# Expert 0's slots emptied by plain transfers, later counts, and another order of each expert's two layers

## The chip, the core and the metric

The kernel runs on one core of a Trainium2 chip. The metric is the device time of one execution in microseconds (us), lower is better: the median of several timed runs. Beside them stands one execution that was recorded by the hardware profiler. The core's engines are PE (TensorE, the matmuls), PEld (its weight loads), DVE (VectorE), ACT (ScalarE), POOL (GpSimd) and SP (SyncE, which here only issues transfers). Each runs its own instructions in order and waits for others at semaphores.

## What is computed

A retention attention, whose output rows are the tokens of a mixture of eight experts with one expert a token:

```python
scores = scale * np.matmul(q, k.transpose(0, 1, 3, 2))      # 8 x 8 heads x 576 x 576
ret = scores * Dmat                                         # decay gamma[h] ** (i - j), causal
x = np.matmul(ret, v)                                       # -> 4608 tokens x 512
logits = x @ w_gate                                         # 8 experts
e_idx = np.argmax(logits, axis=1)
gate_w = softmax(logits)[e_idx]; eom = sigmoid(x @ w_output_gate)
for e in range(8):
    mask = e_idx == e
    h = np.maximum(x[mask] @ w1[e], 0.0)                    # 512 -> 1024
    out[mask] = gate_w[mask, None] * eom[mask, e, None] * (h @ w2[e])   # 1024 -> 512
```

All inputs and outputs are float32.

## The kernel before

**First stage, retention and routing.** A loop of 36 steps goes over tiles `g` of 128 tokens. A step scales v (`prep`, on POOL, one tile ahead), computes scores (also one tile ahead), the output of the tile before by state and by scores, the state's update, and the rows x of the tile before (`xnat`: two PSUM tiles `xa`, `xb`, copied by ACT into `xgrp`; DVE takes the logits into `lg`). Every fourth tile closes a group `n` of four tiles: `gate1a` to `gate3b` find each row's expert and its slot in a DRAM table `xs` of 8 x 4608 slots of 528 words. POOL then writes each tile's 128 rows into `xs` by an indirect transfer (`scatter_x`, L200). The transfers wait in a list, `todo`, and `scatters` issues them, in most steps one, each behind a small `memset`.

An expert works on 616 slots (`CAP`): 360 in a first part (`CA`, tiles t = 0 to 2 of 128, 128 and 104 rows) and 256 in a second (tiles 3 and 4). A slot that no token has must hold an empty row `zx` whose token number is out of bounds. For experts 1 to 7 `fill` computes, from the count of each expert, which slots are empty, and `fill_slots` writes `zx` there by indirect transfers, five for an expert, after all rows are placed. Expert 0 is needed first, so its first part is read while the last tiles are still computed: in `gate4`, after group 5 (`SNAP`), its slots from the count to 360 are filled by three indirect transfers, and later groups go on from slot 360 (`bump`, `base2`). Again after group 7 three such transfers fill up to 616, and then the last group's rows go over filled slots. So in `gate3a` of the last group the copy of the slots into `sli` (L494) waits until all transfers before it have landed (`gt["after"]`).

**Second stage, the experts.** Matmuls run as three float32r products (high x high, high x low, low x high parts). `mm1(e, part, fb)` makes one of eight blocks of the hidden layer for a part of the slots: 12 matmuls of 360 or 256 columns into a PSUM tile `h_ps`; `hidden` (ACT, then DVE) takes it into `hh`, `hl`. `mm2(e, t)` makes a tile of y: 24 matmuls of 512 columns into `y_ps`, ACT scales it, POOL writes its rows to the output by an indirect transfer. The weights of an expert come in four chunks for each layer by SP through three staging buffers `st`, and ACT and DVE split each into high and low part (`load_w`: `hi_w`, `lo_w`) into buffers that each expert uses anew. The next expert's rows come by SP (`load_x`, four transfers a tile into `x_q`), are transposed on DVE and split by ACT and DVE (`transp_hi`, `transp_lo`).

The order of the second stage is written out by hand, and every engine follows it. Expert 0 goes first part of layer one, y of tiles 0 to 2, second part of layer one, y of tiles 3 and 4. Experts 1 to 7 go first part, second part, y of tiles 0 to 4. Their second-layer chunks are loaded within the first part of layer one, the next expert's rows within the second, and its transposes stand ahead of each y tile. Between the stages the counts of all experts (`c_ps`, a matmul of `cum`, L738) are taken within expert 0's first layer. At the end `overflow_table` computes, on DVE, how many rows did not fit; a loop over them closes the kernel.

Of the kernel before, what the change touches and what calls it, by code (L numbers as in the profile page):

```python
# [24 lines left out]
E = 8  # L25
# [23 lines left out]
def tile_retention_moe(  # L49
# [83 lines left out]
    wpool.tile([P, 48], F32, name="shift1")  # L133
# [30 lines left out]
    scat, todo, fillt = [], [], []  # L164
# [34 lines left out]
    def scatter_x(x, at, bound=None):  # L199
        i = G.indirect_dma_start(out=xs, out_offset=bass.IndirectOffsetOnAxis(ap=at, axis=0), in_=x, in_offset=None,  # L200
                                 **({} if bound is None else dict(bounds_check=bound, oob_is_err=False)))
        tc.declare_no_dep(i.ins, group="xs", reason="the slots written differ, and those read so far get no more")
        tc.add_to_no_dep_group("xs", i.ins)
        scat.append(i.ins)

# [258 lines left out]
    def gate2(ps):  # L464

        n, oh, ex, zs = gt["pend"]
        r_ps = ps[:, 0:GT * E].rearrange("p (t e) -> p t e", t=GT)
        T.matmul(r_ps, lhsT=cbf_sb[:, 0, :], rhs=oh, start=True, stop=False, skip_group_check=True)
        if n > 0:
            T.matmul(r_ps, lhsT=cbf_sb[:, 1, :], rhs=cum.rearrange("p (a e) -> p a e", a=1).broadcast_to([P, GT, E]),  # L470
                     start=False, stop=False, skip_group_check=True)
        for t in range(GT - 1):
            T.matmul(r_ps[:, t + 1:], lhsT=cbf_sb[:, 1, :], rhs=oh[:, t:t + 1].broadcast_to([P, GT - 1 - t, E]),
                     start=False, stop=t == GT - 2, skip_group_check=True)
        c_ps = ps[:, GT * E:GT * E + E]
        if n in (SNAP, NTILE // GT - 2):
            T.matmul(c_ps, lhsT=cbf_sb[:, 1, :], rhs=cum, start=False, stop=False, skip_group_check=True)
            for t in range(GT):
                T.matmul(c_ps, lhsT=cbf_sb[:, 1, :], rhs=oh[:, t], start=False, stop=t == GT - 1, skip_group_check=True)
        gt["ps"] = (r_ps, c_ps)  # L480

    def gate3a():
# [5 lines left out]
        if n in (SNAP, NTILE // GT - 2):  # L488
            V.tensor_copy(cnt[:, 0], c_ps[:, 0:1])
# [4 lines left out]
        i = V.tensor_copy(sli, slf)  # L494
        for j in gt.get("after", ()):
            tc.add_manual_dep(i.ins, j.name, SYNC, reason="the last group's rows go over filled slots")
# [19 lines left out]
    def gate3c():  # L516
# [6 lines left out]
        if n in (SNAP, NTILE // GT - 2):  # L523
            gt["fill"] = n

    def gate4():
        n = gt.pop("fill")
        if n == NTILE // GT - 2:

            V.tensor_tensor(out=cnt[:, 0], in0=cnt[:, 0], in1=bump, op=ALU.add)  # L530
            todo.extend(fill(0, 1, cnt[:, 0:1], lim, CT - TA + 1)[0])
        if n == SNAP:

            todo.extend(fill(0, 1, cnt[:, 0:1], float(CA), TA)[0])
            V.tensor_scalar(out=bump, in0=cnt[:, 0], scalar1=-1.0, scalar2=float(CA), op0=ALU.mult, op1=ALU.add)
            V.tensor_scalar(out=bump, in0=bump, scalar1=0.0, scalar2=None, op0=ALU.max)
            V.tensor_copy(base2, base)
            V.tensor_tensor(out=base2[:, 0, 0:1], in0=base2[:, 0, 0:1], in1=bump, op=ALU.add)
# [50 lines left out]
    def scatters(n, pause):  # L589
        for f in todo[0:n]:  # L590

            G.memset(pause, 0.0)
            f()
        del todo[0:n]

    with tc.manual_schedule():
        S_next = scores(0)
        k_rows(0)
        for g in range(NTILE):
# [5 lines left out]
            if g < NTILE - 4:  # L605
                load(g + 4)
            if g == GT * SNAP + 11:
# [13 lines left out]
            if g < NTILE - 1:  # L621

                scatters(2 if GT * SNAP + 6 < g < GT * SNAP + 11 else 1, gap)
# [26 lines left out]
            if g == NTILE - 1:  # L650
                wide = wk.tile([P, H, D], F32, name="vp")
                gate3c()
                gate4()
# [8 lines left out]
    gt["after"] = list(scat)  # L662
# [74 lines left out]
    c_ps = ps_t.tile([P, 512], F32, name="t_ps")[:, 0:E]  # L737
    T.matmul(c_ps, lhsT=cbf_sb[:, 1, :], rhs=cum, start=True, stop=True)  # L738
    V.tensor_copy(cnt[:, :, 0], c_ps)
    V.tensor_tensor(out=cnt[:, 0], in0=cnt[:, 0], in1=bump, op=ALU.add)  # L740
    fills = fill(0, E, cnt, lim, CT)
    fills[0] = fill(0, 1, cnt[:, 0:1], float(CAP), 1, late=True)[0]
# [11 lines left out]
    w = [start_w(1, 1, fp) for fp in range(2)]  # L754
    fill_slots(1)
    fill_slots(0)
    for fb in range(5, FB):
        mm1(0, 0, fb)
# [8 lines left out]
    load_x(1, 1)  # L767
    for e in range(E):
        nx = e + 1 < E
        for fb in range(FB if e > 0 else 0):  # L770

            mm1(e, 0, fb)
            if fb % 2 == 0:
                load_w(2, e, fb // 2)
        for fb in range(FB):
# [10 lines left out]
            elif nx:  # L786
                if fb < CT:
                    load_x(e + 1, fb)
# [8 lines left out]
        xw = {}  # L797
        for t in range(CT):
            if e > 0 or t >= TA:

                for u in range(CT) if e == 0 and t == TA else (t,) if e else ():
                    if nx:
                        xw[u] = transp_hi(e + 1, u)
                        if u > 0:
                            transp_lo(*xw[u - 1])
                        if u == CT - 1:
                            transp_lo(*xw[u])
# [118 lines left out]
```

## Time and profile before

| | us |
|---|---|
| median of 3 timed runs | 603.85 (603.75, 603.85, 605.16) |
| profiled execution, whole | 600.12 |
| its span, first to last instruction | 598.3 |
| busy in the span: PE / PEld | 586.4 / 525.7 |
| busy in the span: DVE / ACT / POOL | 330.8 / 227.0 / 186.3 |
| granted clock of PE, mean share | 0.996 |

The profiled execution was 3.7 us shorter than the median of the timed runs. The busy time of PE is the union of its matmuls' spans; they are pipelined, and the end of each is modelled, so a new matmul starts long before the one ahead has ended. How fast PE goes is therefore read from the starts: how long a stretch of so many matmuls takes.

### The profile page before, as it was taken

How to read it: one execution, taken by the hardware profiler on the slowest of the kernel's cores; microseconds unless marked ns; L12 is line 12 of the kernel's file. 1: busy time of each engine (PE TensorE's matmuls, PEld its weight loads, DVE VectorE, ACT ScalarE, POOL GpSimd, SP SyncE). 2: the span in 40 equal slices, each digit the busy share in tenths (PEclk: the TensorE clock that was granted, in tenths of full speed). 3: DMA queues.
4: the chain of work that ended last, by engine and by line, in shares of the span. 5: the costliest groups of instructions: out<-in, count | busy, mean ns of one | idle time of the engine just before them, and what ended most of it. 6: DMA issues, size and time to landing. Idle time of an engine off the chain costs nothing. (4 is left out here: it accounts for less than half of the span.)

```text
span 598.3 us, 14014 instructions
## 1 busy us (share of the span) xinstructions
PE 586.4 (98%) x5692; PEld 525.7 (88%) x5692; DVE 330.8 (55%) x731; ACT 227.0 (38%) x502; POOL 186.3 (31%) x235
## 2 busy tenths in 40 slices
PE   8999999999999999999999999999999999999995
PEld 6889899889988999889979987997899799889974
DVE  3589899898641864626543472454355435626410
ACT  4534443334322554325333442443344234325210
POOL 3245555575655551125014102501330110110011
PEclk9999999999999999999999999999999999999998
DMA  8889889886235565326424732453273335421011
GB/s 325 293 288 322 323 299 350 328 307 202 92 118 170 173 219 149 141 67 162 172 86 129 183 122 90 125 163 110 89 181 129 121 97 151 131 77 53 1 42 39
DMA packets 54429, 98.97 MB, mean 165 GB/s; under 512 B 14903, under 2 KB 33336, under 8 KB 54364
## 3 DMA queue, kind: packets, MB, share of 16 engines
q1 hardware_dynamic: 44492, 75.42, 39.0%
q0 software_dynamic: 9440, 21.60, 9.9%
q8 instruction: 45, 0.74, 0.5%
q10 hardware_dynamic: 432, 1.05, 0.5%
q14 instruction: 20, 0.16, 0.1%
HBM read 76.45 MB, written 31.18 MB: 180 GB/s over the span
## 5 line engine op out<-in xcount | busy, mean ns | idle before, releaser
L272 PE MATMUL h_ps<-xh,w1h 128*128 128x256 f32 (+1 forms) x512 | 154.7, 302 | 0.0
L272 PE MATMUL h_ps<-xh,w1l 128*128 128x256 f32 (+1 forms) x512 | 154.5, 302 | 0.0
L272 PE MATMUL h_ps<-xl,w1h 128*128 128x256 f32 (+1 forms) x512 | 154.5, 302 | 0.0
L299 POOL DMA_INDIRECT out_dram<-y,idx x40 | 39.8, 995 | 314.3 <-ACT y L298 268.5
L280 DVE SCALAR_TENSOR_TENSOR hl<-h_ps,hh 128x256 fp32r<-128x256 f32 (+1 forms) x128 | 61.1, 477 | 129.1 <-ACT hh L279 125.7
L293 PE MATMUL y_ps<-w2h,hh 128*128 128x512 f32 (+1 forms) x320 | 125.0, 390 | 0.0
L293 PE MATMUL y_ps<-w2l,hh 128*128 128x512 f32 (+1 forms) x320 | 124.9, 390 | 0.0
L293 PE MATMUL y_ps<-w2h,hl 128*128 128x512 f32 (+1 forms) x320 | 124.7, 390 | 0.0
L279 ACT ACTIVATE hh<-h_ps 128x256 fp32r<-128x256 f32 (+1 forms) x128 | 54.8, 428 | 116.9 <-PE h_ps L272 114.8
L272 PEld LDWEIGHTS h_ps<-xh,w1l 128*128 128x128 f32 x512 | 97.1, 190 | 0.0
L272 PEld LDWEIGHTS h_ps<-xh,w1h 128*128 128x128 f32 x512 | 96.1, 188 | 0.3
L272 PEld LDWEIGHTS h_ps<-xl,w1h 128*128 128x128 f32 x512 | 96.1, 188 | 0.3
L298 ACT ACTIVATE y<-y_ps,idx 128x512 f32<-128x512 f32 (+1 forms) x40 | 27.5, 688 | 138.7 <-issue 90.1
L153 DVE TENSOR_TENSOR w1l<-st,w1h 128x512 fp32r<-128x512 f32 x64 | 47.3, 776 | 48.0 <-ACT w1h L148 46.6
L293 PEld LDWEIGHTS y_ps<-w2h,hl 128*128 128x128 f32 (+1 forms) x320 | 58.8, 184 | 14.1
L293 PEld LDWEIGHTS y_ps<-w2h,hh 128*128 128x128 f32 (+1 forms) x320 | 58.8, 184 | 13.7
L293 PEld LDWEIGHTS y_ps<-w2l,hh 128*128 128x128 f32 (+1 forms) x320 | 58.8, 184 | 13.6
L364 POOL TENSOR_TENSOR vp<-pk,con_sb 128x512 f32<-128x512 f32 x36 | 37.5, 1041 | 52.9 <-PE st_ps L404 37.4
L200 POOL DMA_INDIRECT xs<-xgrp,sli x36 | 39.1, 1087 | 29.8 <-issue 12.9
L200 POOL DMA_INDIRECT xs<-zx,fill x42 | 43.3, 1031 | 7.2 <-issue 6.5
L388 DVE TENSOR_TENSOR S_sb<-sc,con_sb 128x512 f32<-128x512 f32 x64 | 41.0, 682 | 7.4 <-PE sc L377 7.0
L153 DVE TENSOR_TENSOR w2l<-st,w2h 128x512 fp32r<-128x512 f32 x64 | 44.7, 736 | 0.0
(130 smaller groups left out, 676.1 us busy)
## 6 DMA issues: line engine op xcount, KB each, us to landing
st<-in_w_dram SPq DMA_DIRECT2D x64, 512.0 KB
pk<-in_pack_dram SPq DMA_DIRECT2D x32, 768.0 KB
x_q<-xs SPq DMA_DIRECT2D x140, 64.0 KB
kn<-in_krow_dram SPq DMA_DIRECT2D x13, 256.0 KB
pk<-in_pack_dram SPq DMA_DIRECT2D x4, 256.0 KB
pk<-in_pack_dram SPq DMA_DIRECT2D x2, 512.0 KB
x_g<-xs SPq DMA_DIRECT2D x4, 256.0 KB
xs<-zx,fill POOLq DMA_INDIRECT x42, 3.6
```

What stands on the lines that cost most here:

```text
L153: V.tensor_tensor(out=lo[:, k], in0=st[:, k], in1=hi[:, k].bitcast(F32), op=ALU.subtract)
L200: i = G.indirect_dma_start(out=xs, out_offset=bass.IndirectOffsetOnAxis(ap=at, axis=0), in_=x, in_offset=None, **({} if bound is None else ...
L272: i = T.matmul(ps, lhsT=a[:, k, :], rhs=b[:, k, 0:n], start=(j == 0), stop=(j == 3 * KB - 1))
L279: A.activation(out=hh, in_=ps, func=AF.Relu)
L280: V.scalar_tensor_tensor(out=hl, in0=ps, scalar=0.0, in1=hh.bitcast(F32), op0=ALU.max, op1=ALU.subtract)
L293: i = T.matmul(ps, lhsT=a[:, n], rhs=b, start=(j == 0), stop=(j == 3 * FB - 1))
L298: A.activation(out=y, in_=ps, func=AF.Copy, scale=idx.bitcast(F32)[0:m, e, t, 1:2])
L299: G.indirect_dma_start(out=out, out_offset=bass.IndirectOffsetOnAxis(ap=idx[0:m, e, t, 0:1], axis=0), in_=y, in_offset=None, bounds_check= ...
L364: G.tensor_tensor(out=vs[g], in0=pk[g][:, 2].rearrange("p (h d) -> p h d", h=H), in1=gk_sb[:, g % CPB].broadcast_to([P, H, D]), op=ALU.mult)
L388: V.tensor_tensor(out=v(S_sb[:, r].rearrange("p a i -> p (a i)")), in0=v(sc[:, r]), in1=cmat_sb[:, 0:2].rearrange("p c a i -> p a (c i)"). ...
```

## The change

It has two parts. **One:** expert 0's 616 slots are written with `zx` by five plain transfers on SP's queue, in steps 3 to 6, before any row is placed; the first row transfer's `memset` waits for them. The two fills of expert 0 within the first stage go, with the count after group 7 and the wait of `sli`; `scatters` issues one transfer a step. The count after group 5 stays, since `bump` needs it. The counts of all experts, and `fill` for experts 1 to 7, come after the last block of expert 0's first part. **Two:** experts 1 to 7 take the order that expert 0 had: y of tiles 0 to 2 stands between the two parts of layer one. The loads of the next expert's rows move into the first part, its transposes stay ahead of the y tiles, and the last two chunks of its first-layer weights come ahead of tiles 3 and 4 instead of 1 and 3.

```diff
+    def empty_rows(t):
+        n = min(P, CAP - P * t)
+        i = SP.dma_start(out=xs[P * t:P * t + n], in_=zx[0:n])
+        tc.add_to_no_dep_group("xs", i.ins)
+        empty.append(i.ins)
...
-        if n in (SNAP, NTILE // GT - 2):
+        if n == SNAP:
             T.matmul(c_ps, lhsT=cbf_sb[:, 1, :], rhs=cum, start=False, stop=False, skip_group_check=True)
...
-        i = V.tensor_copy(sli, slf)
-        for j in gt.get("after", ()):
-            tc.add_manual_dep(i.ins, j.name, SYNC, reason="the last group's rows go over filled slots")
+        V.tensor_copy(sli, slf)
...
     def gate4():
-        n = gt.pop("fill")
-        if n == NTILE // GT - 2:
-            V.tensor_tensor(out=cnt[:, 0], in0=cnt[:, 0], in1=bump, op=ALU.add)
-            todo.extend(fill(0, 1, cnt[:, 0:1], lim, CT - TA + 1)[0])
-        if n == SNAP:
-            todo.extend(fill(0, 1, cnt[:, 0:1], float(CA), TA)[0])
+        gt.pop("fill")
...
     def scatters(n, pause):
         for f in todo[0:n]:
-            G.memset(pause, 0.0)
+            i = G.memset(pause, 0.0)
+            if not scat:
+                for j in empty:
+                    tc.add_manual_dep(i.ins, j.name, SYNC, reason="rows go over empty ones")
             f()
...
+            for t in {3: (0,), 4: (1,), 5: (2, 3), 6: (4,)}.get(g, ()):
+                empty_rows(t)
...
-                scatters(2 if GT * SNAP + 6 < g < GT * SNAP + 11 else 1, gap)
+                scatters(1, gap)
...
+    for fb in range(5, FB):
+        mm1(0, 0, fb)
     c_ps = ps_t.tile([P, 512], F32, name="t_ps")[:, 0:E]
     T.matmul(c_ps, lhsT=cbf_sb[:, 1, :], rhs=cum, start=True, stop=True)
...
     fill_slots(1)
     fill_slots(0)
-    for fb in range(5, FB):
-        mm1(0, 0, fb)
...
+    def next_x(e, u):
+        xw[u] = transp_hi(e + 1, u)
+        if u - 1 in xw:
+            transp_lo(*xw.pop(u - 1))
+        if u in (TA - 1, CT - 1):
+            transp_lo(*xw.pop(u))
     for e in range(E):
         nx = e + 1 < E
-        for fb in range(FB if e > 0 else 0):
-            mm1(e, 0, fb)
-            if fb % 2 == 0:
-                load_w(2, e, fb // 2)
+        if e > 0:
+            for fb in range(FB):
+                mm1(e, 0, fb)
+                if fb % 2 == 0:
+                    load_w(2, e, fb // 2)
+                elif nx:
+                    load_x(e + 1, fb // 2)
+            for t in range(TA):
+                if nx:
+                    next_x(e, t)
+                    if t == 0:
+                        load_x(e + 1, CT - 1)
+                mm2(e, t)
         for fb in range(FB):
             mm1(e, 1, fb)
...
             elif nx:
-                if fb < CT:
-                    load_x(e + 1, fb)
...
-        for t in range(CT):
-            if e > 0 or t >= TA:
+        for t in range(TA, CT):
+            if nx:
                 for u in range(CT) if e == 0 and t == TA else (t,) if e else ():
...
-                if e and nx and t in (1, 3):
-                    load_w(1, e + 1, 2 + t // 2)
-                mm2(e, t)
+                    next_x(e, u)
+                if e:
+                    load_w(1, e + 1, t - 1)
+            mm2(e, t)
```

Three places show how the instructions stand. **DVE in the step after group 5's slots are known** (`S_sb` are scores of a tile, `xT` its output, `w2l` the low part of a weight chunk). Before:

```order
L388 TENSOR_TENSOR S_sb<-sc,con_sb 128x512 x2
L431 TENSOR_TENSOR xT<-o_ps,gq_sb 128x512
L213 TENSOR_TENSOR fl<-cnt,csm_sb 128x3
L215 TENSOR_SCALAR fo<-fl 128x3
L223 TENSOR_TENSOR fl<-fl,fo 128x3
L224 TENSOR_TENSOR fill_2273<-fl,csm_sb 128x3
L535 TENSOR_SCALAR bump<-cnt 128x1
L536 TENSOR_SCALAR bump<-bump 128x1
L537 COPY base_84<-csm_sb 128x8
L538 TENSOR_TENSOR base_84<-base_84,bump 128x1
L153 TENSOR_TENSOR w2l_1944<-st,w2h_1943 128x512
L555 COPY lg<-xa 128x16
```

and with the change:

```order
L395 TENSOR_TENSOR S_sb<-sc,con_sb 128x512 x2
L438 TENSOR_TENSOR xT<-o_ps,gq_sb 128x512
L534 TENSOR_SCALAR bump<-cnt 128x1
L535 TENSOR_SCALAR bump<-bump 128x1
L536 COPY base_84<-csm_sb 128x8
L537 TENSOR_TENSOR base_84<-base_84,bump 128x1
L153 TENSOR_TENSOR w2l_1949<-st,w2h_1948 128x512
L554 COPY lg<-xa 128x16
```

Four instructions of `fill` are gone from between a tile's `xT` and the copy of the logits `lg`. **PE where the counts of all experts are taken** (`t_ps` receives them; `h_ps` belongs to expert 0's first part). Before:

```order
L272 MATMUL h_ps<-xh_2778,w1h_1014 128x360
L272 MATMUL h_ps<-xl_2779,w1h_1014 128x360
L738 LDWEIGHTS cbf_sb
L738 MATMUL t_ps<-cum,cbf_sb 128x8
L272 MATMUL h_ps<-xh_2778,w1l_1015 128x360
L272 MATMUL h_ps<-xh_2778,w1h_1330 128x360
```

and with the change:

```order
L279 MATMUL h_ps<-xl_2765,w1h_1335 128x360
L279 MATMUL h_ps<-xh_2764,w1l_1336 128x360
L754 LDWEIGHTS cbf_sb
L754 MATMUL t_ps<-cum,cbf_sb 128x8
L300 MATMUL y_ps<-w2h_1632,hh_2916 128x512
L300 MATMUL y_ps<-w2l_1633,hh_2916 128x512
```

The matmul of `cum` stood ahead of the last matmul of block 5; now it stands behind block 7, at the border to y. **PE in expert 1**, at the start of its second part of layer one (matmuls of 256 columns). Before:

```order
L272 MATMUL h_ps<-xl_3551,w1h_3420 128x360
L272 MATMUL h_ps<-xh_3550,w1l_3421 128x360
L272 MATMUL h_ps<-xh_3563,w1h_3154 128x256
L272 MATMUL h_ps<-xl_3564,w1h_3154 128x256
L272 MATMUL h_ps<-xh_3563,w1l_3155 128x256
```

and with the change:

```order
L300 MATMUL y_ps<-w2l_3754,hh_3734 104x512
L300 MATMUL y_ps<-w2h_3753,hl_3735 104x512
L279 MATMUL h_ps<-xh_3523,w1h_3092 128x256
L279 MATMUL h_ps<-xl_3524,w1h_3092 128x256
L279 MATMUL h_ps<-xh_3523,w1l_3093 128x256
```

What stands ahead of the 256-column matmuls was a matmul of 360 columns and is one of 512 columns, as in expert 0 before and after.

## Rows read from the trace of the kernel before

**Rows 1.** The page, section 1: busy us, share of the span, instructions.
```profile
PE 586.4 (98%) x5692; PEld 525.7 (88%) x5692; DVE 330.8 (55%) x731; ACT 227.0 (38%) x502; POOL 186.3 (31%) x235
```
**Rows 2.** PE's waits: line, what it waited for: us, times, longest.
```profile
PE t_ps L738 <- DVE cum L522: 1.1, 1, 1.1
PE xa L546 <- DVE lg L555: 0.8, 1, 0.8
```
**Rows 3.** Busy by stretch in the second stage; columns in the first line.
```profile
core 0: us, PE busy (x) PEld busy (x) DVE busy (x) ACT busy (x) POOL busy (x), PEclk, DMA share, GB/s
160.31:166.33 6.02, 6.02 (x39) 5.88 (x38) 3.18 (x13) 1.82 (x6) 4.96 (x7) 1.00 0.25 93
173.87:184.81 10.94, 10.94 (x51) 9.03 (x49) 1.27 (x7) 1.16 (x2) 9.51 (x13) 1.00 0.63 223
191.26:202.15 10.89, 10.89 (x98) 10.89 (x96) 6.50 (x13) 6.31 (x14) 8.22 (x10) 1.00 0.77 226
213.04:228.40 15.36, 15.36 (x97) 15.36 (x96) 8.21 (x15) 8.09 (x16) 10.64 (x12) 1.00 0.58 166
228.40:239.71 11.31, 11.31 (x99) 11.31 (x97) 5.29 (x11) 4.18 (x10) 0.00 (x0) 1.00 0.49 147
239.71:250.60 10.89, 10.89 (x51) 9.00 (x50) 7.75 (x11) 4.27 (x8) 0.98 (x1) 1.00 0.42 154
552.24:563.55 11.31, 11.31 (x98) 11.27 (x97) 4.08 (x9) 3.16 (x8) 0.00 (x0) 1.00 0.01 1
```
**Rows 4.** Order of time near the last group's slots: start, us, engine, line, [idle before].
```profile
168.20 0.33 PE L272 MATMUL h_ps<-xl,w1h 128*128 128x360 f32 x1
168.42 0.17 DVE L494 CAST sli<-slf 128x4 int32<-128x4 f32 x1 [1.14 <-DMA xs<-zx,fill]
169.63 0.18 PE L738 MATMUL t_ps<-cum,cbf_sb 128*128 128x8 bf16 x1 [1.11 <-DVE cum L522]
```
**Rows 5.** Order of time in the step that has the fill of group 5.
```profile
121.32 1.76 DVE L223 TENSOR_TENSOR fl<-fl,fo 128x3 f32<-128x3 f32 x1
122.00 1.05 POOL L364 TENSOR_TENSOR vp<-pk,con_sb 128x512 f32<-128x512 f32 x1
123.17 0.63 PE L404 MATMUL st_ps<-vp,kn 128*64 128x64 f32 x16
124.33 0.17 DVE L555 COPY lg<-xa 128x16 f32<-128x16 f32 x1
124.55 0.76 PE L546 MATMUL xa<-iw,xT 128*128 128x144 f32 x4 [0.75 <-DVE lg L555]
126.03 0.90 PE L377 MATMUL sc<-pk 64*64 64x128 f32 x32 [0.23 <-DVE S_sb L388]
```
**Rows 6.** Order of time at the count after group 7.
```profile
150.57 0.24 PE L479 MATMUL k_ps<-oh,cbf_sb 128*128 128x8 bf16 x4
```
**Rows 7.** Order of time near the first row transfer, on POOL, PE and ACT.
```profile
39.39 1.15 POOL L200 DMA_INDIRECT xs<-xgrp,sli  x1 [2.62 <-PE o_ps L428]
40.56 1.05 POOL L364 TENSOR_TENSOR vp<-pk,con_sb 128x512 f32<-128x512 f32 x1
44.99 1.09 PE L428 MATMUL o_ps<-S_sb,vp 128*64 128x128 f32 x16
48.77 0.35 ACT L550 COPY xgrp<-xa 128x256 f32<-128x256 f32 x1
```
**Rows 8.** Busy by stretch in the first stage, columns as in rows 3.
```profile
16.00:20.00 4.00, 4.00 (x96) 3.62 (x90) 2.15 (x4) 2.45 (x9) 1.04 (x1) 1.00 1.06 391
20.00:24.00 4.00, 4.00 (x88) 3.53 (x82) 2.33 (x5) 3.34 (x13) 1.04 (x1) 1.00 0.29 81
30.00:33.00 3.00, 3.00 (x65) 2.59 (x59) 2.42 (x7) 1.50 (x6) 1.04 (x1) 1.00 0.55 171
```
**Rows 9.** Order of time in experts 7 and 1: a chunk's last split, SP's row loads.
```profile
551.53 1.30 DVE L153 TENSOR_TENSOR w2l<-st,w2h 128x512 fp32r<-128x512 f32 x2
217.87 9.88 SPq L168 DMA_DIRECT2D x_q<-xs  x20
```

More of the change, by code (lines that the diff above doesn't have):

```diff
@@ L128, in load_rest @@
             G.memset(zx.bitcast(I32)[:, DM:DM + 1], NT)
-    wpool.tile([P, 48], F32, name="shift1")
+    wpool.tile([P, 64], F32, name="shift1")
     W1, W2 = {}, {}
@@ L163, in tile_retention_moe @@
     pe = [None]
-    scat, todo, fillt = [], [], []
+    scat, todo, fillt, empty = [], [], [], []
     pools = {"xt0": xta, "ht0": hpa}
@@ L487, in gate3a @@
         V.tensor_tensor(out=sl, in0=r_ps, in1=bs.broadcast_to([P, GT, E]), op=ALU.add)
-        if n in (SNAP, NTILE // GT - 2):
+        if n == SNAP:
             V.tensor_copy(cnt[:, 0], c_ps[:, 0:1])
@@ L522, in gate3c @@
         V.tensor_tensor(out=cum, in0=cum, in1=ohs, op=ALU.add)
-        if n in (SNAP, NTILE // GT - 2):
+        if n == SNAP:
             gt["fill"] = n
     def gate4():
-        n = gt.pop("fill")
-        if n == NTILE // GT - 2:
-            V.tensor_tensor(out=cnt[:, 0], in0=cnt[:, 0], in1=bump, op=ALU.add)
-            todo.extend(fill(0, 1, cnt[:, 0:1], lim, CT - TA + 1)[0])
-        if n == SNAP:
-            todo.extend(fill(0, 1, cnt[:, 0:1], float(CA), TA)[0])
[L535 to L538, printed above, removed]
+        gt.pop("fill")
+        V.tensor_scalar(out=bump, in0=cnt[:, 0], scalar1=-1.0, scalar2=float(CA), op0=ALU.mult, op1=ALU.add)
+        V.tensor_scalar(out=bump, in0=bump, scalar1=0.0, scalar2=None, op0=ALU.max)
+        V.tensor_copy(base2, base)
+        V.tensor_tensor(out=base2[:, 0, 0:1], in0=base2[:, 0, 0:1], in1=bump, op=ALU.add)
     def xnat(g):
@@ L652, in tile_retention_moe @@
                 gate3c()
-                gate4()
                 scatters(len(todo), wide)
@@ L661, in tile_retention_moe @@
                 transp_lo(*x)
-    gt["after"] = list(scat)
     psctx.close()
@@ L736, in tile_retention_moe @@
     weights_lo(NTILE)
[L737 to L742, printed above, removed]
     rest.__exit__(None, None, None)
@@ L754, in tile_retention_moe @@
     w = [start_w(1, 1, fp) for fp in range(2)]
+    for fb in range(5, FB):
+        mm1(0, 0, fb)
+    c_ps = ps_t.tile([P, 512], F32, name="t_ps")[:, 0:E]
+    T.matmul(c_ps, lhsT=cbf_sb[:, 1, :], rhs=cum, start=True, stop=True)
+    V.tensor_copy(cnt[:, :, 0], c_ps)
+    V.tensor_tensor(out=cnt[:, 0], in0=cnt[:, 0], in1=bump, op=ALU.add)
+    fills = fill(0, E, cnt, lim, CT)
+    fills[0] = fill(0, 1, cnt[:, 0:1], float(CAP), 1, late=True)[0]
     fill_slots(1)
     fill_slots(0)
-    for fb in range(5, FB):
-        mm1(0, 0, fb)
     load_idx(1, 0)
@@ L767, in tile_retention_moe @@
     load_x(1, 1)
+    xw = {}
+    def next_x(e, u):
[4 more added lines that the diff above has]
+            transp_lo(*xw.pop(u))
     for e in range(E):
         nx = e + 1 < E
-        for fb in range(FB if e > 0 else 0):
-            mm1(e, 0, fb)
-            if fb % 2 == 0:
-                load_w(2, e, fb // 2)
+        if e > 0:
[11 more added lines that the diff above has]
+                mm2(e, t)
         for fb in range(FB):
@@ L796, in tile_retention_moe @@
             overflow_table()
-        xw = {}
-        for t in range(CT):
-            if e > 0 or t >= TA:
+        for t in range(TA, CT):
+            if nx:
                 for u in range(CT) if e == 0 and t == TA else (t,) if e else ():
[L802 to L807, printed above, removed]
-                if e and nx and t in (1, 3):
-                    load_w(1, e + 1, 2 + t // 2)
-                mm2(e, t)
+                    next_x(e, u)
+                if e:
+                    load_w(1, e + 1, t - 1)
+            mm2(e, t)
     mctx.close()
```

## The prediction

> **What bounds the kernel now.** I read the page's first section, then PE's waits, then the busy time by stretch, and last the order of time around each wait. The first shows PE busy for 98% of the span [rows 1]; all other engines have room. So only two things can shorten the span: a gap in PE's chain that closes, or a stretch of the same matmuls that takes PE less time. PE's list of waits has few entries, and two of them lie where the change works: 1.1 us for `cum` and 0.8 us for `lg` [rows 2]. No wait at all is listed within experts 1 to 7, so there the reader should look at how long equal stretches take. The clock that PE was granted is 1.00 in every stretch used here [rows 3], the higher of its two levels.
>
> The stretch table holds the surprise. The second part of layer one is 96 matmuls of 256 columns in each expert. In expert 0 they take 10.89 us (113 ns each), in expert 1 and in expert 7 11.31 us (118 ns each) [rows 3]. Experts 2 to 6 read 11.30 or 11.31 in the same view. Code, tiles and clock are the same. It isn't other work in the way: expert 0's stretch is the busiest (DMA share 0.77, POOL 8.22 us) and the fastest, expert 7's the quietest (0.01 and 0) and slow. What differs is what PE did before: in expert 0 a tile of y (512 columns), in the others 360-column matmuls. The first part shows the same kind of thing: 36 matmuls of 360 columns behind 144-column ones of `xnat` take 6.02 us (167 ns each), 96 behind a tile of y take 15.36 us (160 ns each) [rows 3]. I read this as a state that a stretch takes over at its start and keeps: how far the weight loads run ahead of the matmuls. That reading is an inference; the times are measured.
>
> **The change, part by part.**
>
> *The last group's wait goes.* `sli` waited 1.14 us for the last transfer of `zx`; behind it on DVE came the sum into `cum`, for which PE stood still: its matmuls start at 168.20 and then at 169.63 [rows 4]. A normal step is 0.16 us, so 1.27 us are lost. Without fills in the list `sli` waits for nothing that is late, and the matmul of `cum` now comes behind block 7, 25 steps of 0.16 us or 4 us after the place where `cum` was late by 1.3 us. What is late next is nothing on PE: the blocks need only `xh`, `xl` and PSUM tiles freed long before. The move has no price of its own, since the matmul interrupts the stream once in either place. Gain 1.27 us; at least 1.1, the listed wait.
>
> *The fill after group 5 goes.* In this step DVE spends 1.76 us on `fl<-fl,fo`, a copy of 3 columns, while POOL scales a tile beside it [rows 5]. That pushes the logits' copy to 124.33, and PE, done with its state update at 123.80 (123.17 + 0.63), starts `xa` only at 124.55 and waits 0.23 us once more for the scores' tile [rows 5]. The instruction goes with three others. Then `lg` comes at 122.6 or earlier, 1.2 us ahead of PE. Gain 0.75 + 0.23 = 0.98 us. Four instructions for `bump` stay; should one of them be held for 1.6 us in the same way, `lg` comes at 124.2 and 0.2 us of the gain are left. I take 0.98, since in this step POOL now issues one transfer fewer and scales its tile earlier.
>
> *Five small matmuls after group 7 go.* Four of them span 0.24 us with their pipeline [rows 6]; I take 0.1 us.
>
> *Five plain writes come, 1.3 MB in steps 3 to 6.* At the 391 GB/s that this stage reaches they are 3.3 us of transfer. The queue has room: the DMA share is 0.29 in the four us from 20 and 0.55 in the three from 30, which leaves 2.8 + 1.4 = 4.2 us [rows 8]. Behind them on SP stand the loads of tiles and weight chunks; on POOL, behind the first `memset` that now waits, stand the first row transfer and the scaling for tile 9. That transfer began at 39.39 and the scaling ended at 41.61; PE needs it at 44.99, and ACT overwrites the transferred rows at 48.77 [rows 7]. So the writes may land up to 3.4 us later than the first transfer used to begin before PE sees it. The room exceeds the writes, so I take 0; bound 0 to 2 us of loss.
>
> *Fewer transfers on POOL.* Six row transfers and their memsets leave POOL's queue. POOL is not waited for there, so nothing by itself.
>
> *The counts and fills of all experts come later.* They need `cum` and DVE, and POOL then writes the slots of expert 1 while PE makes y of tiles 0 to 2. These transfers were bound by POOL, busy 9.51 of 10.94 us in that stretch [rows 3], and its row transfers ahead of them now start earlier. Their reader is the load of expert 1's rows, which PE needs at 213.04 [rows 3], almost 30 us after that stretch. I take 0.
>
> *The other order in experts 1 to 7.* The 256-column stretch now follows a tile of y, as in expert 0. If the state is taken over as I read it, each expert gains 11.31 - 10.89 = 0.42 us, seven of them 2.94 us. The y tiles 0 and 1 now follow 360-column matmuls: expert 0 did that in 10.94 us, expert 1 behind 256 columns in 10.89 [rows 3], so up to 0.05 x 7 = 0.35 us go back; I take 0.15 us, because expert 0's came from the slower 360-column state. That is 2.8 us, between 2.6 and 2.9. If the state isn't the reason, it is 0.
>
> What covers this order: y of tile 0 now begins 11.3 us earlier against the second-layer chunks. In expert 7 the last chunk's low part was ready at 552.83 (551.53 + 1.30) [rows 9]; in the new place y begins where the first part ends, 552.24 [rows 3], and reads this chunk 18 matmuls of 0.23 us later, at 556.3. The cover is 3.5 us. The transposes for part one move ahead by a whole y stretch against their reader, those of part two are now read after the next expert's first part: more cover than before.
>
> Sum: 1.27 + 0.98 + 0.1 + 2.8 = 5.15 us. The profiled execution, 600.12 us with 1.8 us around its span of 598.3, would become 595.0. The median of the timed runs lies 3.7 us above it; I take the same difference for the change: 603.85 - 5.15 = 598.7 us.
>
> **Rivals.** *The 256-column matmuls keep their 118 ns.* Then the order gives nothing: 1.27 + 0.98 + 0.1 = 2.35 us, 601.5 us. For it: expert 0 is the only example of the fast stretch. Against it: the quiet expert 7 is slow, and the 360-column stretches show two rates as well. On this the Trainium skill, page "TensorE: Matmul & The Clock Gate", section "Back-to-back issue gap", speaks against a gain: it gives the gap between matmuls as the column count over the clock plus a constant (262 cycles at 256 columns), with no term for what ran before. By that rule the order would be worth 0, and the sum 2.35 us. The trace differs from it, with 113 and 118 ns for the same column count at the same clock.
>
> *The early writes stall POOL or the tile loads.* They land more than 3.4 us late, PE waits for a scaled tile or for the rows' buffer. Each us beyond the cover costs one; at 1 to 3 us lost the time is 599.7 to 601.7.
>
> *One of the two waits doesn't go* (a `bump` instruction is held in place of the fill, or `cum` is late for another reason): 599.7 to 600.0.
>
> *Slower: the second-layer weights come late.* On SP's queue the next expert's row loads now stand between the chunks' loads. Twenty of them took 9.88 us to issue [rows 9], so the twelve ahead of the fourth chunk are 5.9 us. If all of them queue up between the first chunk's split and the fourth chunk's load, the chunk is 5.9 - 3.5 = 2.4 us late in each of seven experts: 16.8 us lost against 5.15 gained, 615.5 us. It decides from 3.5 + 5.15 / 7 = 4.2 us of delay on. Against it: the row loads depend on buffers that are free before the expert begins, and the fourth chunk waits for a staging buffer anyway, so that they should pass while SP would wait.
>
> **How the numbers follow.** Forecast 598.7: 0.66. 118 ns kept, 601.5: 0.17. Early writes, 599.7 to 601.7: 0.08. One wait left, about 599.9: 0.04. Late weights, slower: 0.05. The range must take in 601.5 to leave out no more than 2 in 10: its upper end is 602.0, its lower end 597.9, the best case of the bounds (5.35 us) less what timed runs scatter downwards. A measurement of this kernel can tell about 0.3%, 1.8 us. The forecast lies 5 us below, and even the first rival 2.35 us, of which I put a third into "same". Faster 0.85, same 0.10, slower 0.05.
>
> **What would show it.** In the profile after: the 256-column stretches of experts 1 to 7 at 10.9 us each; PE's waits without `cum` and without `lg`; no DVE instruction of a few columns that takes over 1 us just after group 5; no wait of PE, and none of `vp` for a `gap`, in steps 7 to 10. Wrong would be 11.3 us stretches behind y, a PE wait for `w2l`, or waits between 36 and 50 us.

## The result, and the profile after

The changed kernel takes 610.31 us (609.06 to 611.13, six runs) against 604.12 for the kernel before on the same chip: 1.0097 times as long, 95% interval 1.0083 to 1.0111. On a second chip it is 604.13 against 599.53, 1.0069 (1.0046 to 1.0091). I had forecast 598.7 us, faster. Chips differ by some 5 us in both kernels, so each ratio below is to the kernel before on the same chip. The profiled execution of after has a span of 609.0 us.

What I had worked out for TensorE's waits and for the order of the experts is in the trace. PE's waits in the profile after (line, what it waited for, us, times, longest), to be set against [rows 2]:

```profile
PE k_ps L365 <- DMA con_sb<-in_cmat_dram: 1.6, 1, 1.6
PE o_ps L426 <- issue: 1.5, 6, 0.4
PE sc L561 <- DVE zx L558: 1.5, 1, 1.5
PE st_ps L411 <- issue: 0.8, 1, 0.8
PE o_ps L435 <- issue: 0.5, 2, 0.3
PE sc L384 <- DVE S_sb L395: 0.2, 1, 0.2
```

The waits for `cum` and for `lg` are gone. PE's busy time by stretch after, to be set against [rows 3]:

```profile
core 0: us, PE busy (x), PEclk, DMA share, GB/s
196.46:207.35 10.89, 10.89 (x97) 1.00 0.83 251
218.25:233.61 15.36, 15.36 (x98) 1.00 0.81 240
233.61:244.50 10.89, 10.89 (x50) 1.00 0.25 93
250.00:260.88 10.88, 10.88 (x98) 1.00 0.15 46
571.15:582.04 10.89, 10.89 (x97) 1.00 0.07 20
```

The 256-column stretches of experts 1 and 7 (250.00 and 571.15) now take 10.88 and 10.89 us, as expert 0's always did; the first y tile behind 360-column matmuls (233.61) takes 10.89. From the first matmul of layer one to PE's last matmul it is 431.32 us, in the kernel before 435.81. Yet the span grew. The page's first section shows it as a fall of PE's share, with the busy time almost unchanged from [rows 1]:

```profile
PE 587.0 (96%) x5687; PEld 524.9 (86%) x5687; DVE 328.6 (54%) x720; ACT 227.5 (37%) x502; POOL 180.3 (30%) x223
```

The time lies behind PE's last matmul. That stretch in the kernel before, then after (columns as in [rows 3]):

```profile
591.19:598.30 7.11, 0.00 (x0) 0.00 (x0) 0.00 (x0) 0.69 (x1) 0.98 (x1) 0.65 0.07 26
```

```profile
593.21:609.00 15.79, 0.00 (x1) 0.00 (x0) 0.00 (x0) 0.69 (x1) 0.99 (x1) 0.66 0.03 13
```

ACT scales the last tile (0.69 us), POOL issues the last transfer (0.98), and then nothing counts as busy: 7.1 us in all before, 15.8 us after. The instructions of the program's last lines show who holds the end; POOLq is GpSimd's sequencer, and the columns are count, shortest/median/longest ns, first and last start. Before, then after:

```profile
L818 POOLq INC_SWDGE_SEM  x1: 408/408/408, 592.7 to 592.7; - x1
...
L922 POOLq DRAIN  x3: 40/103/1047, 596.4 to 598.0; - x3
```

```profile
L830 POOLq INC_SWDGE_SEM  x1: 2403/2403/2403, 594.8 to 594.8; - x1
...
L934 POOLq DRAIN  x3: 40/103/9312, 598.8 to 608.7; - x3
```

GpSimd's DRAIN at the kernel's end takes 9.31 us instead of 1.05, and all engines wait for it; the `INC_SWDGE_SEM` that closes the skipped loop over overflow tiles takes 2.40 us instead of 0.41, which puts the DRAIN's start 0.4 us further from PE's end (5.63 us after it instead of 5.23). Together 8.7 us. No step of my prediction looked there.

This execution of after lost more in its first stage: layer one begins at 161.89 us (155.38 before), with 12 places where PE's next instruction starts 0.25 to 0.98 us after the one before it. In the 15 later profiles of kernels with this part of the change it begins at 153.9 to 157.7, so most of that belongs to the execution or to its chip. What caused it there stays open.

### The profile page after: what moved, and what is told of

The parts are those of the page before. It is cut to its first block, busy times and chain, and to the rows that moved or that the text cites. A ratio compares the mean times of both kernels' runs of the same rounds, so it can differ in the third digit from the quotient of the medians.

```text
span 609.0 us, 13992 instructions
## 1 busy us (share of the span) xinstructions
PE 587.0 (96%) x5687; PEld 524.9 (86%) x5687; DVE 328.6 (54%) x720; ACT 227.5 (37%) x502; POOL 180.3 (30%) x223
## 3 DMA queue, kind: packets, MB, share of 16 engines
q10 hardware_dynamic: 432, 1.05, 0.5%
## 5 line engine op out<-in xcount | busy, mean ns | idle before, releaser
L371 POOL TENSOR_TENSOR vp<-pk,con_sb 128x512 f32<-128x512 f32 x36 | 38.8, 1078 | 61.1 <-PE st_ps L411 41.8
L153 DVE TENSOR_TENSOR w1l<-st,w1h 128x512 fp32r<-128x512 f32 x64 | 45.8, 752 | 8.6 <-ACT w1h L148 7.2
L260 DVE TENSOR_TENSOR xl<-x_t,xh 128x512 fp32r<-128x512 f32 x35 | 23.7, 678 | 41.4 <-ACT xh L256 40.5
L153 DVE TENSOR_TENSOR w2l<-st,w2h 128x512 fp32r<-128x512 f32 x64 | 43.4, 715 | 0.0
```

What stands on the lines that cost most here:

```text
L153: V.tensor_tensor(out=lo[:, k], in0=st[:, k], in1=hi[:, k].bitcast(F32), op=ALU.subtract)
L260: V.tensor_tensor(out=lo, in0=src, in1=hi.bitcast(F32), op=ALU.subtract)
L371: G.tensor_tensor(out=vs[g], in0=pk[g][:, 2].rearrange("p (h d) -> p h d", h=H), in1=gk_sb[:, g % CPB].broadcast_to([P, H, D]), op=ALU.mult)
```

## The experiments

**Each half alone, and both kernels again.** The edits: the kernel before with the new loop over the experts (order only); the changed kernel with the old loop (slots only).

> The kernel before, unchanged, for the spread of its own profile: the one profiled execution of it that stands in the case (600.12 us, span 598.3) is 4 us under the median of its timed runs (604.12), while the profiled execution of the changed kernel (610.92) lies at its median. Theory A (the profiled execution of before was a lucky one): a new profile has a span of about 602.5, with the first matmul of layer one some 3 to 4 us later than 155.38, because PE stops in the middle of groups of matmuls in the first stage, as it does in the changed kernel. Theory B (the 4 us lie in the end of the program): layer one begins at 155.4 again and GpSimd's last DRAIN takes 3 to 5 us instead of 1.05.

> The changed kernel, unchanged, for the spread of its own profile. If what was seen in its first profile belongs to the program, then layer one begins at 161.9 us again (within 0.5), the same 10 to 12 matmul groups o_ps<-pk,stT stop in their middle for 0.3 to 0.6 us, and GpSimd's last DRAIN takes 9.3 us again. If it belongs to the execution, layer one begins somewhere between 155 and 161 and the DRAIN may take 1 us.

> The kernel before with the second part of the change alone: in experts 1 to 7 three tiles of y between the two parts of layer one. Theory 1 (the loss belongs to the slots of expert 0; the order only gives): 604.1 - 2.8 = 601.3 us, the 256-column stretches at 10.9 us, GpSimd's last DRAIN as short as before. Theory 2 (the long DRAIN at the end, 8.3 us, comes with the order, since the last experts' work and the transfers before the end lie differently): 604.1 - 2.8 + 8.3 = 609.6 us.

> The changed kernel with the loop over the experts as it was: the first part of the change alone (plain writes to expert 0's slots, one row transfer a step, counts later). Theory 1 (the whole loss belongs to this part): 610.3 + 2.8 = 613.1 us, layer one begins at about 162 us, and the last DRAIN takes 9.3 us. Theory 2 (the DRAIN comes with the order of the experts): 613.1 - 8.3 = 604.8 us, with a DRAIN of about 1 us; the stops in the first stage stay.

| Kernel | ratio to before (95%) | layer one begins | to PE's last matmul | from there to the end |
|---|---|---|---|---|
| before again | 0.9993 (0.9979 to 1.0007) | 154.71 | 436.20 | 7.04 |
| after again | 1.0069 (1.0046 to 1.0091) | 156.18 | 431.32 | 15.76 |
| order only | 0.9951 (0.9934 to 0.9967) | 156.55 | 432.06 | 7.09 |
| slots only | 1.0122 (1.0102 to 1.0141) | 154.63 | 434.50 | 15.67 |

(The three right columns are us of the profiled execution.) The long end is the slots' alone; slots only shows it in the same rows:

```profile
L820 POOLq INC_SWDGE_SEM  x1: 2402/2402/2402, 590.7 to 590.7; - x1
...
L924 POOLq DRAIN  x3: 40/103/9214, 594.8 to 604.5; - x3
```

Theory 1 held for both halves in where the long end lies, by the difference to before on this chip (-2.6 and +7.3 us). For slots only it missed the rest: it expected 9.0 us more than before and layer one at about 162 us, which came at 154.63. For the repeat of before neither theory held: its timed median here is 599.54 us, so its profile and its times agree here; what made the 4 us between them on the first chip stays open. In the repeat of after the DRAIN came back within 1 ns, the 12 stops did not.

**Is it the number of GpSimd's transfers?** The change takes six row transfers away, 118 to 112. Eight is the number of semaphores that these transfers use in turn, and 112 is a multiple of it; that and a limit between 112 and 118 were the theories. The edit repeats `k` transfers of fills in experts 2 and 3 (`k` = 1, 6, 8):

```diff
     def fill_slots(e):
-        for f in fills[e]:
-            G.memset(iw, 0.0)
+        for n, f in enumerate(fills[e] + fills[e][0:more.get(e, 0)]):
+            i = G.memset(iw, 0.0)
+            if n >= CT:
+                tc.add_manual_dep(i.ins, scat[-CT].name, SYNC, reason="the same rows again")
             f()
```

The fourth kernel has 18 more `G.memset(iw, 0.0)` in expert 2's fill instead, and no more transfers.

> The changed kernel with one more row transfer on GpSimd: the first five rows groups' fill of expert 2 is followed by a repeat of its first transfer, in the experts, where GpSimd has room. 113 transfers instead of 112. Theory C (the long end goes with the count: after 112 transfers = 14 x 8 the last instructions use the first of the eight semaphores in rotation, S[111], after 113 the second): INC_SWDGE_SEM takes 0.4 us and the last DRAIN 1.0 us, and the time is 8.7 us under that of the changed kernel, 0.75% under the kernel before (about 595.4 where before is 599.5). Theory D (a threshold or a ring of transfers between 112 and 118, or the place in GpSimd's instructions): the DRAIN stays at 9.3 us, and the time 0.7% above before.

> The changed kernel with six more row transfers, 118 as in the kernel before (five repeats in expert 2, one in expert 3). Theories C and D both expect the short end: INC_SWDGE_SEM 0.41 us, DRAIN 1.05 us, 0.7% under the kernel before. If the end stays long (9.3 us), the number of transfers isn't the cause, and the order of the last instructions or GpSimd's code is.

> The changed kernel with eight more row transfers, 120 = 15 x 8. Theory C (remainder by eight): the end is long again, INC_SWDGE_SEM 2.4 us on S[111] and DRAIN 9.3 us. Theory D (a threshold between 112 and 118): short, 0.4 and 1.05 us.

> The changed kernel with 18 more memsets on GpSimd in the experts and no more transfers: GpSimd's instructions then stand as far along as in the kernel before (which has 18 more of them), with 112 transfers. If the long end comes from the place in the instruction stream, INC_SWDGE_SEM and DRAIN are short (0.4 and 1.05 us); if it comes from the number of transfers, they stay at 2.4 and 9.3 us.

One more (113): 1.0076 (1.0054 to 1.0098). Six more (118): 0.9963 (0.9939 to 0.9987), with a DRAIN of 1.05 us and 7.09 us from PE's last matmul to the end. Eight more (120): 597.17, a single time. Memsets (112): 603.73, a single time, with before at 599.63. The rows of one more, of eight more, and of the memsets:

```profile
L834 POOLq INC_SWDGE_SEM  x1: 2433/2433/2433, 588.9 to 588.9; - x1
...
L938 POOLq DRAIN  x3: 40/103/9296, 593.0 to 602.8; - x3
```

```profile
L834 POOLq INC_SWDGE_SEM  x1: 442/442/442, 589.9 to 589.9; - x1
...
L938 POOLq DRAIN  x3: 40/103/1211, 593.1 to 594.9; - x3
```

```profile
L832 POOLq INC_SWDGE_SEM  x1: 2407/2407/2407, 587.6 to 587.6; - x1
...
L936 POOLq DRAIN  x3: 40/103/9214, 591.7 to 601.4; - x3
```

The remainder by eight falls twice (113 long, 120 short), and the place in GpSimd's instructions falls (memsets). Left is a limit between 113 and 118. The six repeats in two lumps were not free: five in a row in expert 2's fill made PE wait 1.7 us for `hl` in layer one, so that PE's part took 433.50 us instead of 431.32.

**Where the limit is, and what it counts.** The repeats now stand one in each of the experts 2 to 7 (or fewer); the last kernel's repeats have 16 rows.

```diff
+        for n, f in enumerate(fills[e] + fills[e][0:1 if e > 1 else 0]):
...
-            f()
+            (f if n < CT else partial(scatter_x, zx[0:16], f.args[1][0:16], E * NT - 1))()
```

> The changed kernel with six more row transfers on GpSimd, 118 as before, but one in each of the experts 2 to 7 (a repeat of the first transfer of that expert's fill) instead of five in one place, where the five in a row cost TensorE 1.7 us at expert 3's h_ps and 2.2 us in all. Both theories of the end (a count or the descriptors that the transfers write) expect the short end: INC_SWDGE_SEM 0.41, DRAIN 1.05, 7.1 us from TensorE's last matmul to the end instead of 15.7. From layer one's first matmul to TensorE's last 431.3 us as in the changed kernel. Time: 8.7 us under the changed kernel's (ratio 1.007 to 1.010 to before), so 0.992 to 0.995 of the kernel before.

> The changed kernel with two more transfers (114), in experts 2 and 3, to find where between 113 (long end) and 118 (short end) the change lies. A count with the limit just above 113 gives a short end (1.05 us). If the limit is in what the transfers write, 16 queues' worth of rows each, with eight transfers of 104 rows that write less than the others, 114 is still short of it, and the DRAIN stays at 9.3 us.

> The changed kernel with four more transfers (116), in experts 2 to 5. Together with the kernel of 114 it halves the interval: a short end (DRAIN 1.05 us) puts the limit at 116 or below, a long one (9.3 us) at 117 or 118.

> The changed kernel with six more transfers as in the spread version, but each of 16 rows instead of 128: 118 transfers, with about as much written as by 113. If the number of transfers decides, the end is short (INC_SWDGE_SEM 0.41, DRAIN 1.05). If the descriptors that they write decide (a transfer of 16 rows writes about a fifth of one of 128 on each of the 16 DMA engines: the page counts 5 packets an engine for 128 rows), the end stays long (2.4 and 9.3 us).

Six spread: 595.70 us, 0.9931 of before (0.9916 to 0.9946), PE's part 431.32 us, the end 7.09: faster than both kernels. 114 and 116 took 597.09 and 597.33 (single times), with ends of 7.91 and 6.85 us; the six small ones took 604.21 with 16.30 (before: 599.46). The rows of 114 transfers, and of 118 with six small ones:

```profile
L832 POOLq INC_SWDGE_SEM  x1: 323/323/323, 590.2 to 590.2; - x1
...
L936 POOLq DRAIN  x3: 40/103/721, 593.6 to 594.8; - x3
```

```profile
L832 POOLq INC_SWDGE_SEM  x1: 2524/2524/2524, 587.6 to 587.6; - x1
...
L936 POOLq DRAIN  x3: 45/103/9712, 591.8 to 602.1; - x3
```

So the limit lies between the 113th and the 114th full transfer, and of the two expectations for 114 the plain count held. The small ones show that what a transfer writes counts towards it all the same (118 transfers, limit not reached), while the DRAIN grows with their number: 9712 - 9214 = 498 ns for six, 83 ns each. (The 9214 ns stand in all three other kernels with 112; the two profiles of after show 9312 and 9311, and these 98 ns stay open.)

The 114th transfer can be found in every kernel that has one, in the kernel before too. Order of time there, on POOL and on ACT, in the kernel before:

```profile
571.85 0.99 POOL L299 DMA_INDIRECT out_dram<-y,idx  x1 [32.77 <-issue]
575.82 0.98 POOL L299 DMA_INDIRECT out_dram<-y,idx  x1 [2.98 <-ACT y L298]
```

```profile
569.41 0.69 ACT L298 ACTIVATE y<-y_ps,idx 128x512 f32<-128x512 f32 x1 [5.28 <-PE y_ps L293]
574.86 0.69 ACT L298 ACTIVATE y<-y_ps,idx 128x512 f32<-128x512 f32 x1 [4.76 <-PE y_ps L293]
```

A y tile's transfer begins 0.27 to 0.30 us after ACT has scaled the tile (575.82 - 575.55 for the 115th). The 114th begins 571.85 - 570.10 = 1.75 us after: 1.47 us late, with "issue" as the releaser. The same 1.75 us stands at the 114th transfer with 118 in the spread version, with 120, and with 114 in all, where it is the last one and so on the path to the end. In the last 12 transfers of the kernel with 112, none is late.

**The other direction, the law, the unit, and what is left of the first stage.** The edits: the kernel before without the last of five transfers in the fills of experts 2 to 7 (112); the changed kernel with only the first two of these five (94); the changed kernel with three more transfers of 16 rows in each of the experts 2 to 7 (130); slots only with the six spread transfers (118).

```diff
-        for f in fills[e]:
+        for f in fills[e][0:4 if e > 1 else CT]:      # kernel before, 112
+        for f in fills[e][0:2 if e > 1 else CT]:      # changed kernel, 94
```

> The kernel before with six transfers fewer: in the experts 2 to 7 the last of the five transfers of each expert's fill is left out (it covers slots that stay unused with this data; the work of 6 transfers is left out, none of TensorE's). 112 transfers instead of 118, nothing else changed. If the number of transfers alone makes the long end: INC_SWDGE_SEM 2.4, DRAIN 9.2 to 9.3, 15.7 us from TensorE's last matmul to the end instead of 7.1, and the time 8.7 us (1.45%) over that of the kernel before. If something else in the changed kernel is needed as well (the plain writes, the later counts), the end stays at 7.1 us and the time the same.

> The changed kernel with 18 transfers fewer: in the experts 2 to 7 only the first two of five transfers of each fill are made (the rest covers slots unused with this data). 94 transfers. If the end costs in proportion to the transfers since the start (from 112 to 113 the DRAIN grew by 0.08 us, from 114 to 120 by 0.49): DRAIN 0.06 + 94 x 0.0817 = 7.7 us and INC_SWDGE_SEM 0.03 + 94 x 0.0212 = 2.0 us. If the long end is a fixed price: 9.3 and 2.4 us again.

> The changed kernel with 18 more transfers of 16 rows each, three in each of the experts 2 to 7: 130 transfers. With six small ones the limit was not reached. If a small transfer takes a share of the limit by what it writes on each DMA engine (a row and a closing entry, 2 against 9 of a full one; room left after 112 full ones is under two full ones, 18 entries at most), it is reached after 5 to 9 more of the small ones' worth, in the last ten transfers or so: short end, DRAIN 0.7 to 1.4 us. If only full transfers count, it isn't: DRAIN 0.06 + 130 x 0.0817 = 10.7 us.

> The first part of the change alone (plain writes, one row transfer a step, counts later; experts in the old order) with the six more transfers in the experts, so that the end is short: what the waits of the first stage are worth. By the prediction: 1.27 + 0.98 + 0.1 = 2.35 us under the kernel before, 0.9961 of it. Rival (the step of group 5's fill gets 1.1 us shorter, but PE stops elsewhere, after the plain writes and in the step behind, and gives most of it back): 1.3 us, 0.998.

The kernel before with 112 transfers is 608.33 us, 1.0168 of before (1.0126 to 1.0209): the number alone makes the long end. With 94 the DRAIN is 7.74 us and the `INC_SWDGE_SEM` 2.04 us, as the proportional law said (600.75 us, a single time). With 18 small ones the limit is reached, the end is 6.31 us long, and the single time is 595.42 (before 599.85). Rows of 112 in the kernel before, of 94, and of 18 small ones:

```profile
L818 POOLq INC_SWDGE_SEM  x1: 2402/2402/2402, 592.7 to 592.7; - x1
...
L922 POOLq DRAIN  x3: 40/103/9214, 596.8 to 606.5; - x3
```

```profile
L830 POOLq INC_SWDGE_SEM  x1: 2043/2043/2043, 586.7 to 586.7; - x1
...
L934 POOLq DRAIN  x3: 40/103/7744, 590.2 to 598.4; - x3
```

```profile
L832 POOLq INC_SWDGE_SEM  x1: 377/377/377, 588.6 to 588.6; - x1
...
L936 POOLq DRAIN  x3: 45/103/892, 591.6 to 593.1; - x3
```

From 94 to 112 transfers the DRAIN grows by (9214 - 7744) / 18 = 81.7 ns each; from 114 to 120, past the limit, by (1211 - 721) / 6 = 81.7 ns each. Nothing is left at zero transfers but 7744 - 94 x 81.7 = 64 ns. By the same line 721 ns stand for 8 transfers after 114, 1047 for 12 after 118, 892 for 10 after 130 with small ones, where the 128th is the late one (1.94 us after its y). I read this as a list of transfers that GpSimd goes through at the end, and which is cut down to the last eight or so when a room that the transfers fill is full. The numbers are measured, the list is an inference.

The room holds 113 full transfers, or 109 full and 18 small ones, but not 114, and not 110 and 18. So 18 small ones take the room of 3 to 5 full ones, a small one 0.17 to 0.28 of a full one; by rows alone it would be 1/8. By the packets in the profile, five on each DMA engine for a full transfer (those of 104 rows too) and two for a small one, it would be 0.4. That falls as well: 109 and 18 make 581 packets on an engine and fit, 114 make 570 and don't. The Trainium skill, page "DMA: Bandwidth & Descriptors", section "The descriptor swizzle", tells of eight data entries and one that closes on each DMA engine for a transfer to 128 partitions. By an estimate from that page a small one would be 2/9 = 0.22, which lies within the measured bounds: 1020 entries (112 full and six small) fit, 1026 (114 full, or 110 and 18 small) don't.

Slots with a short end come to 0.9978 of before (0.9967 to 0.9989), 1.36 us. The rival expectation (1.3) held, mine (2.35) did not. The place is the step with group 5's fill and the one behind it. Its rows in slots with 118 (the profile of after has stops of its own there), to be set against [rows 5]:

```profile
120.95 0.66 DVE L536 COPY base<-csm_sb 128x8 f32<-128x8 f32 x1
122.40 0.16 DVE L554 COPY lg<-xa 128x16 f32<-128x16 f32 x1
```

```profile
123.49 0.76 PE L545 MATMUL xa<-iw,xT 128*128 128x144 f32 x4
```

The longest of the four instructions for `bump` takes 0.66 us, `lg` starts 1.1 us ahead of PE's next `xa` (I had worked out 1.2), and the step takes 3.93 us in the 15 later profiles (4.57 in the first of after) where it took 5.05. But the next one takes 4.66 to 6.46 us in the kernels with the change, 4.97 to 5.25 in most, where it took 4.34 (4.59 once). In slots with 118:

```profile
125.93 1.09 PE L435 MATMUL o_ps<-S_sb,vp 128*64 128x128 f32 x14
127.30 0.27 PE L435 MATMUL o_ps<-S_sb,vp 128*64 128x128 f32 x1 [0.27 <-issue]
```

PE stops in the middle of 16 matmuls that wait for nothing. Counted in the records of PE's own instructions (weight loads, matmuls and those of its sequencer), this stop stands at position 5314 in each of the 13 profiles that have it. The other stops without a releaser in the first stage, before and after, stand at 707, 1219, 1474, 1730, 2243, 2499, 3523, 4291 and 6083 (eleven of the twelve in the first profile of after apart): all 194 or 195 more than a multiple of 256. In the records of the DMA queues PE's instructions arrive as packets of 16 KB, 45 of them, and each of these stops ends 1.1 to 1.7 us after one has landed. I read it as PE out of instructions. In the four profiles that still wait for `lg`, PE comes to the same position 1.4 to 1.7 us after its packet has landed and doesn't stop. So the wait seems to have covered this place; without it the stop shows. The Trainium skill, page "Runtime: NRT & Kernel Launch", section "Instruction fetch mechanics", gives the same blocks of 16 KiB, 256 instructions, and calls the cost of crossing one mostly hidden. The trace agrees on the block and on "mostly": of some two dozen such places in the first stage one to four stop PE in a profile. Those stops, 0.3 to 2.0 us from one start to the next, aren't hidden.

**The stop in step 9.** A second stop, at position 1474, comes with the slots. In the four kernels without them the packet before it starts 1.0 to 1.4 us ahead of the scores of step 8, and step 9 takes 3.93 us. In the kernels with them it starts between 0.1 us ahead and 1.5 us behind, and the step takes 3.93 to 5.42 us, longer the later the packet: 4.07 at 0.1 us, 4.34 at 0.3, 4.6 at 0.7 to 0.9, 4.90 at 1.0, 5.42 at 1.5. Do the plain writes hold it up? The edit moves them a step:

```diff
-            for t in {3: (0,), 4: (1,), 5: (2, 3), 6: (4,)}.get(g, ()):
+            for t in {2: (0,), 3: (1,), 4: (2, 3), 5: (4,)}.get(g, ()):
```

> The changed kernel with six more transfers in the experts (118) and its five plain writes one step earlier: in steps 2 to 5 instead of 3 to 6. Theory (the plain writes hold up the packet of TensorE's instructions that starts at 36.0 to 37.6 us with them and at 34.4 to 35.5 in the kernels without): the packet starts below 35.5, step 9 takes 3.93 us without a stop at L411, and the time is about 0.5 us under that of the kernel with the writes in steps 3 to 6, which the timing alone can hardly tell. Rival (something else in the first steps, or the earlier writes hold up the tile loads instead): the stop of 0.4 us or more stays, or a wait for pk shows in steps 4 to 8.

> The changed kernel with six more transfers in the experts, again, as the partner on the same chip: 0.993 of the kernel before as in its first run (0.9916 to 0.9946), the packet of instructions at 36 us or later, and a stop of TensorE in step 9 or 10.

Early: 595.51 us, 0.9941 (0.9919 to 0.9963), the packet 0.7 us behind, step 9 at 4.60 us. Partner: 595.07, 0.9923 (0.9910 to 0.9936), 0.2 us behind, 4.07 us. POOL's first `memset` stands still for 2.0 to 4.4 us, mostly for the plain writes, in the 15 other profiles with them (4.40 in the first of after); with the earlier writes it starts at 36.34 us without a wait. So the writes do land earlier, and PE's stop stays. The theory isn't borne out: one step earlier changes nothing for the better. That the packet is late with this half of the change is shown; which transfer it stands behind stays open.

## Why the prediction was wrong

- **The sign: "Fewer transfers on POOL. [...] nothing by itself."** This is the step that failed. It asked only who waits for POOL while PE works. Six transfers fewer leave the count at 112, what I read as the settling at the 114th never comes, and GpSimd's DRAIN goes through all 112: +8.7 us behind PE's last matmul. My way of reading, PE's chain and its gaps, took the 7.1 us behind it as given. The one late transfer of the kernel before, 1.75 us against 0.28, stood in the trace that I had; I didn't ask what it was.
- **The last group's wait, 1.27 us: right.** Layer one's start to PE's end went from 435.81 and 436.20 us (before, twice) and 436.01 (before with 112 transfers) to 434.50 with the slots alone: 1.3 to 1.7. In the new order it went from 432.06 to 431.32, 0.7 us; there PE's wait for `cum` had been 0.5 us, not 1.1 to 1.5.
- **The fill after group 5, 0.98 us: right in its step, wrong in the sum.** The step gained 1.12 us and `lg` is early, as worked out. I named nothing that would be late next but `lg`; it was PE's own instructions (as I read the stops), and the step behind gave some 0.6 to 0.9 of it back in most kernels. The five small matmuls (0.1) can't be told apart in this.
- **The plain writes, 0, bound 0 to 2 us: within the bound, by another way.** The first row transfer begins at 41.59 instead of 39.39 us [rows 7], at 38.8 to 40.9 in the later profiles, and PE never waits for what POOL scales, so the cover that I named held. But step 9 takes 0.1 to 1.5 us more in 15 of 16 profiles. Together with the step behind group 5's this accounts for 1.36 us having come instead of 2.35.
- **The order in experts 1 to 7, 2.8 us: right.** 434.50 - 431.32 = 3.2 us by the profiles; by times, order only is 0.9951 of before, 2.6 us of medians. The 256-column stretches are at 10.88 to 10.89 us in all seven. The 0.15 us that I took for y behind 360 columns did not come: an expert's y tiles take 16.39 + 10.89 us instead of 27.31, a little less. The times show that the order makes the difference; the state that I named, how far weight loads run ahead, no run tested. The rival by the rule in the Trainium skill, page "TensorE: Matmul & The Clock Gate", section "Back-to-back issue gap" (which that page gives for a single matmul by itself), falls: at the same clock 256 columns go at 113 ns behind y and at 118 behind 360 columns.
- **The other rivals.** No wait for second-layer weights. For tile loads PE waits 0.4 to 0.7 us in four of the 16 profiles, at 11 us, before the first plain write is issued (13 to 17 us), so not for the writes. The slower rival was the wrong one: I put 0.05 on "slower" for late weights and nothing on the end. The 5.35 us of the best case are a slip in the sum: the bounds that I gave add up to 1.27 + 0.98 + 0.1 + 2.9 = 5.25. Nothing hangs on it.

Put together, on the second chip, in us against before: order -3.2, `cum` -1.3 to -1.7, the rest of the first stage about 0, the end +8.7. That is +3.8 to +4.2; the medians say +4.6. On the first chip they say +6.2, and its profile has the 12 stops besides.

## What to carry to other kernels

Price the end of the program like any other stage: what lies between TensorE's last matmul and the last instruction, who holds it, and what that depends on; a change in the number of transfers on GpSimd can move it by 8.7 us with every engine else unchanged. Here 118 full transfers, six of them made for no other reason, beat 112 by some 8 us, and 0.992 to 0.993 of the kernel before is the best version found. Where a wait on PE goes, look at what it covered: here it seems to have given PE's own instructions time to arrive.

## What the hardware showed that I had not expected

- GpSimd's last DRAIN costs 81.7 ns for each software-made transfer that is still on its account, from 0.72 us (114 transfers) to 9.7 us (118, six of them small), and `INC_SWDGE_SEM` about 20 ns each: (2402 - 2043) / 18.
- At the 114th full transfer GpSimd is 1.47 us late, and from there on the DRAIN is short (I read this as an account that is settled there); 16-row transfers reach this place later.
- TensorE can stop at a fixed place in its blocks of 256 instructions, 0.3 to 2.0 us, in the first stage, where matmuls are small and the DMA share is 0.5 to 1.05 in stretches of 10 us; in the experts it didn't.
